# A gated attention and state-space mix on one core: an emission order planned with the matrix engine's instruction blocks, half of a Hankel table copied by one DMA, and earlier keys

## The chip, the cores and the metric

The kernel runs on one core of one Trainium2 chip. The time is that of one execution on the device, in microseconds (us). A profile is one further execution, recorded by the hardware profiler. The engines are called as the profile calls them: PE is the matrix engine (PEld its weight loads), DVE the vector engine, ACT the scalar engine, POOL the general engine, SP the engine that only issues transfers.

## What is computed

Two branches read the same x (2048 rows of 448, bf16) and are mixed by a gate per row. Branch A is attention with 16 query heads of width 28 that share one key and one value head. Branch B is a state-space layer: a kernel K of length 2048 for each of 448 channels, made from 256 complex modes, convolved causally with x.

```
q = (x @ wq) per head;  k = x @ wk;  v = x @ wv
a = softmax(q k^T * 28**-0.5) v, heads joined, @ wo
P = exp(dt*A*l) for l in 0..2047
K[d,l] = Re sum_n C[d,n] P[d,n,l] dt*B[d,n]
b = causal_conv(K, x) per channel + x * Dskip
out = g*a + (1-g)*b,  g = sigmoid(x . gate_w)
```

## The kernel before

**Order.** The code doesn't write its instructions in the order in which they run. Each call of `op` or `dma` records an operation with a guess of its duration, its dependences and a priority `pr` (smaller goes first). `schedule` then plays a list schedule: again and again it takes, of all operations whose inputs are there, the one that can start earliest by the guesses, and appends it to its engine's list. `emit` writes the lists out and puts semaphore waits where one engine needs another. So a guess that changes moves instructions on every engine, and an engine never overtakes its own list: an instruction that waits holds up all that stand behind it.

**Attention.** There are 1024 score tiles: 16 blocks of queries i (4 heads of one group by 512 queries) times 16 key tiles times 4 heads. A tile is 128 keys by 512 queries in one PSUM bank. The tiles go in sets of 3 and 2 by turns over five banks (`main`, `sets`). For each set PE makes the scores, ACT takes the exponential of the whole set from PSUM into a ring of 15 tiles in SBUF (`expT`, L1115), and PE multiplies them with the values (`pv`, L1125). A set's scores come in one of two forms. In the row form (L1084) a tile is one matmul over 29 rows of the array, from qT. In the full form (L1093) a tile is four matmuls over 128 rows and 32 columns each, from qM, a copy of qT in which each head has its own 32 rows and the rest are zero; POOL issues the four DMAs that fill it. Before, sets of 3 use the row form, sets of 2 the full form, and block i = 0 the row form throughout, so that no qM is made for it.

**Query shift.** `prep_x` transposes x, makes the keys kT in four quarters q (PE, then ACT at L587, then a maximum on DVE at L590), and from the four maxima the bias matrix Wb (L607, L609). Each `qproj(i)` needs Wb for its last matmul (L750), so the first scores wait for the fourth quarter of kT. The transposed x of quarters 2 and 3 lies in qM until it is stored to a scratch tensor; POOL then clears qM (L605).

**State space.** `masters` and `tables` build powers of the modes on DVE for groups of 32 channels (14 groups c); the last operation of a group's table is L854. `kgen(c)` is 128 small matmuls (L871) on PE; DVE copies the result (L881, L884), and POOL stores it to the scratch tensor KP by nine DMAs. `tload` loads Toeplitz blocks of KP, 1 MiB for a group index gi (0 to 111), four DMAs of 256 KB each from SP, into seven buffers (four in T, three in the part of U that is used up). `conv` (L930, two of them for a group, each over four gi) multiplies them with U; DVE takes the result out (L939), PE turns it (L950), DVE adds it to O (L958). U holds x in a Hankel form for all 128 partitions; it is assembled from x by DMAs into a staging buffer in O and 16 copies on POOL (L520). PE's fillers `kgen`, `conv` and the turns have priorities 1.7, 1.6 and 1.55 and go between the score sets. A filler (`ni` set and `pr` at least 1) is held back when the instructions issued lately are over BURST.

**End.** After the last exponential come the normalisation of block 15 (L985, L1003 to L1018), the last output projections (L1036, added to O at L976), what is left of `conv`, and the stores of O, which stand behind the last table load on SP.

## Time and profile before

| what | us |
| --- | --- |
| median of 3 runs (566.47 to 568.52) | 567.91 |
| the profiled execution, time | 568.51 |
| its span, first to last instruction | 566.6 |
| ACT busy in the span | 487.0 (86%) |
| PE busy | 469.7 (83%) |
| DVE busy | 462.3 (82%) |
| POOL busy | 174.1 (31%) |

A line of the profile gives line, engine, operation and tile, then how often, the busy time and the mean of one in ns, and after the last bar the idle time of the engine just before these instructions with what ended most of it. In a timeline, the two first numbers are start and length, and the bracket at the end is the idle time before, with what ended it. "issue" there means that the engine waited for nothing that the profile shows.

### The profile page before, as it was taken

To read this page: it belongs to the slowest core of one execution; us is meant where nothing else is said; L and a number is where in the kernel's file an instruction comes from. 1 tells how busy PE (TensorE), PEld (TensorE's weight loads), DVE (VectorE), ACT (ScalarE), POOL (GpSimd) and SP (SyncE) were. 2 spreads that over 40 slices of the span, in tenths; PEclk is the share of its full clock that TensorE was granted. 3 is DMA by queue.
4 is the path that set the end of the run, shared out by engine and by line. 5 is a ranking of instruction groups with operands and counts; after the bars stand their busy time and mean duration, and the time that the engine had idled before them with its cause. 6 is when DMAs were issued, how large, how long until landed. Compare 5 with 4: busy or idle time off the path is not lost.

```text
span 566.6 us, 20978 instructions
## 1 busy us (share of the span) xinstructions
PE 469.7 (83%) x9383; PEld 228.7 (40%) x9383; DVE 462.3 (82%) x826; ACT 487.0 (86%) x431; POOL 174.1 (31%) x317
## 2 busy tenths in 40 slices
PE   5678878879779989799887999879878999889772
PEld 4522112315325444434444443534424453545351
DVE  4877999999889999799898999879898997871230
ACT  3779999999899999799898999879998997999700
POOL 2026531512414233044323352142321450152200
PEclk8855578879889999999899999989999997999985
DMA  8932251187369899979899599957989499868998
GB/s 256 219 86 74 67 141 45 30 309 228 116 202 294 279 346 290 309 259 308 272 356 301 189 352 307 349 191 242 321 273 347 123 360 359 305 187 296 357 386 271
DMA packets 92322, 141.68 MB, mean 250 GB/s; under 512 B 23156, under 2 KB 30940, under 8 KB 92232
## 3 DMA queue, kind: packets, MB, share of 16 engines
q1 hardware_dynamic: 82360, 130.32, 69.3%
q0 software_dynamic: 9216, 9.46, 6.8%
q8 instruction: 73, 1.20, 0.9%
q10 hardware_dynamic: 656, 0.57, 0.4%
q14 instruction: 17, 0.14, 0.1%
HBM read 129.68 MB, written 5.28 MB: 238 GB/s over the span
## 4 chain that ended last, share of the span: by engine, by line
ACT 52%; PE 30%; DMA 6%; issue 5%; DVE 3%; SPq 3%; ACTq 0%
ACT expT L1115 51%; PE psS L1093 5%; PE psS L1084 5%; PE psB L1125 4%; SPq L134 3%; PE psX L871 3%; DMA U<-KP_scratch 2%; DMA T<-KP_scratch 2%; PE psS L871 2%; PE psS L930 2%; PE psX L930 2%; PE psS L741 1%; DMA seedw<-in_gate_w_dram 1%; PE psS L1036 1%; PE psX L950 1%
## 5 line engine op out<-in xcount | busy, mean ns | idle before, releaser
L1115 ACT ACTIVATE expT<-psS 128x1536 bf16<-128x1536 f32 (+1 forms) x410 | 468.8, 1304 | 34.8 <-PE psS L1084 21.7
L1093 PE MATMUL psS<-qM,kT 128*32 128x512 bf16 x1532 | 126.9, 406 | 11.4 <-ACT expT L1115 9.7
L1084 PE MATMUL psS<-qT,kT 29*128 29x512 bf16 x641 | 94.8, 422 | 32.1 <-ACT expT L1115 27.8
L1125 PE MATMUL psB<-expT,vaug 128*32 128x512 bf16 x1024 | 111.2, 416 | 5.3 <-issue 3.4
L134 POOL DMA_DIRECT2D KP_scratch<-kstg x126 | 67.7, 545 | 78.3 <-DVE kstg L884 71.5
L832 DVE TENSOR_TENSOR tab<-tab,mbf 128x2048 bf16<-128x2048 bf16 (+4 forms) x70 | 68.5, 979 | 1.0
L1084 PEld LDWEIGHTS psS<-qT,kT 29*128 29x128 bf16 x641 | 21.6, 92 | 92.0 <-ACT expT L1115 78.4
L1125 PEld LDWEIGHTS psB<-expT,vaug 128*32 128x32 bf16 x1024 | 27.8, 96 | 62.8 <-issue 49.1
L134 POOL DMA_DIRECT2D rdenB<-R_scratch x60 | 29.9, 504 | 54.6 <-DMA R_scratch<-denT 44.3
L1093 PEld LDWEIGHTS psS<-qM,kT 128*32 128x32 bf16 x1532 | 29.2, 99 | 40.3 <-ACT expT L1115 30.3
L871 PE MATMUL psS<-tab 128*32 128x64 bf16 x1024 | 41.1, 287 | 5.1 <-issue 4.9
L930 PE MATMUL psS<-T,U 128*26 128x128 bf16 (+7 forms) x1408 | 34.2, 228 | 6.9 <-DMA T<-KP_scratch 4.8
L871 PE MATMUL psX<-tab 128*32 128x64 bf16 x768 | 33.0, 286 | 8.0 <-issue 7.9
L134 POOL DMA_DIRECT2D qM<-qT x60 | 30.3, 513 | 25.4 <-DVE qT L753 12.2
L834 DVE TENSOR_TENSOR tmp<-tab,mbf 128x256 bf16<-128x256 bf16 (+3 forms) x56 | 36.1, 644 | 0.0
L930 PE MATMUL psX<-T,U 128*26 128x128 bf16 (+7 forms) x1376 | 34.3, 225 | 1.9 <-issue 1.8
L871 PEld LDWEIGHTS psS<-tab 128*32 128x32 bf16 x1024 | 30.5, 135 | 13.3 <-issue 7.2
L134 POOL DMA_DIRECT2D denT<-acc x15 | 11.7, 782 | 73.4 <-DVE acc L985 73.4
L930 PEld LDWEIGHTS psS<-T,U 128*22 128x22 bf16 (+7 forms) x1408 | 26.4, 97 | 19.4 <-DMA T<-KP_scratch 5.9
L849 DVE TENSOR_TENSOR tab<-tab,tmp 128x4096 bf16<-128x4096 bf16 x14 | 32.0, 2288 | 0.3
L834 DVE TENSOR_TENSOR tab<-tab,mbf 128x4096 bf16<-128x4096 bf16 x14 | 31.9, 2281 | 0.0
L930 PEld LDWEIGHTS psX<-T,U 128*26 128x26 bf16 (+7 forms) x1376 | 26.5, 97 | 13.2 <-issue 5.0
(155 smaller groups left out, 591.6 us busy)
## 6 DMA issues: line engine op xcount, KB each, us to landing
T<-KP_scratch SPq DMA_DIRECT2D x348, 256.0 KB, 5.7
U<-KP_scratch SPq DMA_DIRECT2D x100, 256.0 KB, 5.7
rdenB<-R_scratch POOLq DMA_DIRECT2D x60, 64.0 KB, 5.0
qM<-qT POOLq DMA_DIRECT2D x60, 32.0 KB, 5.0
tab<-in_A_x_dram SPq DMA_DIRECT2D x4, 448.0 KB, 5.9
O<-in_A_x_dram SPq DMA_DIRECT2D x16, 112.0 KB, 2.6
O<-cst SPq DMA_DIRECT2D x1, 1792.0 KB, 9.3
KP_scratch<-kstg POOLq DMA_DIRECT2D x112, 16.0 KB
```

The costliest lines, as they stand in the source:

```text
L134: return [e.dma_start(o, i, **kw) for o, i in pairs]
L741: pg.op("pe", lambda e, T=T: e.matmul(px(), self.Wq.v(0, DT, T * 512 + g * 128, [[1, 128]]), self.xT.v(0, DT, T * 512, [[1, 512]]), start= ...
L832: vo(lambda e, dst=dst, src=src, mr=mr: e.tensor_tensor(dst, src, mr, ALU.mult), 2 * n, done + mk(lv), [kr, ki])
L834: vo(lambda e, src=src, mi=mi, w=w, tb=tb, to=to: e.tensor_tensor(tb.v(0, P, to, [[w * EW, 2], [EW, w], [1, EW]]), src, mi, ALU.mult), 2 * ...
L849: vo(lambda e: e.tensor_tensor(tab.v(0, P, FM, [[64, 2], [EW, 32], [1, 64]]), tab.v(0, P, lo + 31 * EW, [[BLK, 2], [-EW, 32], [1, 64]]), r ...
L871: r = e.matmul(G.v(32 * g, 32, 64 * jj, [[1, 64]]), tab.v(0, P, lo + comp * BLK + 64 + o, [[EW, 32]]), tab.v(0, P, fo, [[mo - fo, 2], [EW, ...
L930: r = e.matmul(ps.v(32 * j, 32 - 2 * n, 128 * k, [[1, 128]]), self.U.v(0, P, (4 * gi + j) * 32 + 2 * n, [[1, 32 - 2 * n]]), tbuf.v(0, P, t ...
L950: r = e.matmul(px.v(64 * par, 64, 64 * k, [[16, 4], [1, nt]]), self.cst.v(0, P, cs * 512 + 128 * k + 64 * (1 - mu), [[1, 64]]), self.ident ...
L1084: r = e.matmul(self.psS.v(0, P, 512 * b, [[1, 512]]), kT.v(32 * h, DH + 1, 128 * kt, [[1, 128]]), qT.v(32 * h, DH + 1, 512 * (i % 2), [[1, ...
L1093: r = e.matmul(self.psS.v(32 * j, 32, 512 * b, [[1, 512]]), kT.v(0, P, 128 * kt + 32 * j, [[1, 32]]), self.qM.v(0, P, (i % 2) * XQ + 512 * ...
L1115: pg.op("act", lambda e: e.activation(expT.v(0, P, 512 * es[0], spread(es, n)), self.psS.v(0, P, 512 * bs[0], spread(bs, n)), AF.Exp, scal ...
L1125: r = e.matmul(self.psB.v(32 * h, 32, 0, [[1, 512]]), vaug.v(0, P, 32 * kt, [[1, 32]]), expT.v(0, P, 512 * ring[t], [[1, 512]]), start=(kt ...
```

## The change

The planner's guesses change. PE's instructions are counted (a matmul is two: weight load and multiplication), and an instruction of block j of 256 can't start before that block has been fetched; a fetch starts when PE enters the block before it, and takes 5300 ns while DMAs run and 3300 ns otherwise. Fillers are further held back so that the scores behind them don't run dry. PE's durations are multiplied by 1.8 between 21 and 45 us of the plan. Transfers get a new cost formula, and one exponential of `prep_params` a longer duration.

```diff
-    BURST, FETCH = 250, 4000.0
+    BLOCK, FIRST, FETCH, IDLE, NEED = 256, 172, 5300.0, 3300.0, 0.015
+    HALF = (21000.0, 45000.0, 1.8)
...
-                    if o.ni and o.pr >= 1:
...
+                    if e == "pe":
+                        j = (npe + o.ni - self.FIRST - 1) // self.BLOCK + 1
+                        if j < len(block):
+                            r = max(r, block[j])
+                            if o.pr >= 1 and block[-1] > r:
+                                left = self.FIRST + (len(block) - 2) * self.BLOCK - npe - o.ni
+                                r = max(r, block[-1] - left / self.NEED)
...
+            if e == "pe":
+                npe += o.ni
+                while npe > self.FIRST + (len(block) - 2) * self.BLOCK:
+                    block.append(r + (self.FETCH if dmafree > r else self.IDLE))
```

The work itself changes in five places. The upper half of U (64 of the 128 partitions) is no longer loaded and copied but taken from the lower half by one DMA of 28,672 pieces of 32 bytes; POOL's copies fall from 16 to 8, and all of U is first cleared by one DMA. The transposed x of quarters 2 and 3 lies in the ring `expT`, so qM is cleared by POOL at the very start. qM is made for block 0 as well; the first six sets use the row form, sets 6 to 13 the full form, and the later ones the old rule (3 row, 2 full). The keys get priority -2, ahead of the sines of `prep_params`. `kgen` gets priority 1.4, ahead of `conv` and the turns. Each gi of `tload` is loaded by two DMAs of 512 KB (the even and the odd partitions) in place of four.

```diff
+        for k in range(2):
+            pm(V(self.qM, k * XQ, XQ), 0.0, 1800, [("qM", k)], 1.5)
...
+        self.late.append(pg.dma([(V0(self.U, 0, 32 * D, 64), Z(32 * D, 64))], (8192, 448), "zU", rd=[("cst", 1)],
+                                wr=[("U", k) for k in range(4)] + uc, pr=0.25).i)
         for k in range(2):
...
+        half = lambda o: bass.AP(tensor=self.U.h, offset=o, ap=[[2 * rs, 64], [32, D], [1, 16]])
+        pg.dma([(half(rs + 16), half(0))], (28672, 32), "du", rd=[("U", 0), ("U", 1)],
+               wr=[("U", 2), ("U", 3)] + uc, pr=0.35, slow=True)
...
-                rd=[("b", b), "s0"], wr=[("kT", q)])
+                rd=[("b", b), "s0"], wr=[("kT", q)], pr=-2)
...
-            if q >= 2:
-                pg.op("pool", lambda e, xT=xT, xo=xo: e.memset(xT.v(0, P, xo, [[1, XQ]]), 0.0), 2500,
-                      wr=self.xk(q) + [("qM", q % 2)], pr=1)
...
-        return ((self.xT, 0), (self.T, NTR * TW + 768 - XQ), (self.qM, 0), (self.qM, XQ))[q]
+        return ((self.xT, 0), (self.T, NTR * TW + 768 - XQ), (self.expT, 9 * 512), (self.expT, 5 * 512))[q]
...
-        if i:
+        if True:
...
-                      wr=[X, "kst", "kst2"], pr=1.7, lock=G if jj == 0 and comp == 0 else None)
+                      wr=[X, "kst", "kst2"], pr=1.4, lock=G if jj == 0 and comp == 0 else None)
...
-        for j in range(4):
-            lst.append((buf.v(0, P, o + 1024 * j, [[1, 1024]]), dram(self.KP, (4 * gi + j) * KW, [[1, 64], [KH, 2], [1, 1024]])))
+        for h in range(2):
+            to = bass.AP(tensor=buf.h, offset=h * buf.rs + o, ap=[[2 * buf.rs, 64], [1024, 4], [1, 1024]])
+            lst.append((to, dram(self.KP, h * KH + 4 * gi * KW, [[1, 64], [KW, 4], [1, 1024]])))
...
-            if len(ts) == 3 or dec(ts[0])[0] == 0:
+            if s < 6 or s >= 14 and len(ts) == 3:
```

**Where it moves instructions.** The changed file has 18 or 19 more lines ahead of these places, so its line numbers are higher by that much. First ACT's list around the first exponentials, before: L698 and L699 are the sines, L587 is the fourth quarter of the keys, L706 the decay factors mq, L1115 the exponentials of the scores.

```order
L698 ACTIVATE T<-T 128x896
L699 ACTIVATE T<-T,small 128x896
L703 ACT_TABLE_LOAD
L703 ACTIVATE mbf<-T 128x896
L587 ACTIVATE kT<-psS,small 128x512
L618 ACTIVATE gt<-psB 128x16
L706 ACTIVATE mq<-T 128x2x14x32 x5
L1115 ACTIVATE expT<-psS 128x1536
```

The same place now:

```order
L716 ACTIVATE T<-T 128x896
L606 ACTIVATE kT<-psS,small 128x512
L717 ACTIVATE T<-T,small 128x896
L721 ACT_TABLE_LOAD
L721 ACTIVATE mbf<-T 128x896
L636 ACTIVATE gt<-psB 128x16
L724 ACTIVATE mq<-T 128x2x14x32 x3
L1134 ACTIVATE expT<-psS 128x1536
L1134 ACTIVATE expT<-psS 128x1024
L1134 ACTIVATE expT<-psS 128x1536
L724 ACTIVATE mq<-T 128x2x14x32
```

The fourth quarter of the keys has moved ahead of the second sine, a table load and an exponential, and two of the five mq now stand behind the first exponentials. Next PE's list where the first `kgen` (L871) begins, before: L1084 and L1093 are scores, L1125 the product with the values, L741 and L750 the next query block.

```order
L741 MATMUL psX<-xT,Wq 128x512
L871 MATMUL psS<-tab 32x64 x8
L1084 MATMUL psS<-qT,kT 128x512 x3
L1125 MATMUL psB<-expT,vaug 32x512 x4
L871 MATMUL psS<-tab 32x64 x8
L1093 MATMUL psS<-qM,kT 32x512 x8
L750 MATMUL psX<-qT,Wb 128x512
L871 MATMUL psS<-tab 32x64 x16
```

The same place now:

```order
L889 MATMUL psS<-tab 32x64 x8
L1112 MATMUL psS<-qM,kT 32x512 x8
L1144 MATMUL psB<-expT,vaug 32x512 x4
L889 MATMUL psS<-tab 32x64 x24
L1103 MATMUL psS<-qT,kT 128x512 x3
L1144 MATMUL psB<-expT,vaug 32x512 x4
L889 MATMUL psS<-tab 32x64 x8
L1112 MATMUL psS<-qM,kT 32x512 x8
L889 MATMUL psS<-tab 32x64 x32
```

Counted over the whole list, the first `kgen` began behind 130 score tiles and now begins behind 108; the last one (c = 13) ran from tile 975 to 995 and now runs from 940 to 955; each ends 25 to 47 tiles sooner, and takes 12 to 18 tiles where it took 15 to 32. Last DVE's list from the normalisation of block 15 on, before: L1007 to L1018 belong to it, L976 adds the output projection to O, L939 and L958 take one `conv` out.

```order
L1007 RECIPROCAL denT<-psS 128x16
L1009 COPY rdenB<-denT 128x512
L1018 TENSOR_TENSOR onT<-acc,psS 128x512
L976 SCALAR_TENSOR_TENSOR O<-psS,gt,O 128x448 x2
L939 TENSOR_TENSOR cst<-psX,omq 128x512
L976 SCALAR_TENSOR_TENSOR O<-psS,gt,O 128x448 x2
L958 TENSOR_TENSOR O<-O,psX 128x16x16
L939 TENSOR_TENSOR cst<-psS,omq 128x512
L958 TENSOR_TENSOR O<-O,psX 128x16x16
L939 TENSOR_TENSOR cst<-psS,omq 128x512
L958 TENSOR_TENSOR O<-O,psX 128x16x16
```

The same place now:

```order
L1026 RECIPROCAL denT<-psS 128x16
L1014 TENSOR_TENSOR onT<-acc,rdenB 128x512
L1028 COPY rdenB<-denT 128x512
L1037 TENSOR_TENSOR onT<-acc,psS 128x512
L995 SCALAR_TENSOR_TENSOR O<-psS,gt,O 128x448 x2
L958 TENSOR_TENSOR cst<-psS,omq 128x512
L995 SCALAR_TENSOR_TENSOR O<-psS,gt,O 128x448 x2
L977 TENSOR_TENSOR O<-O,psS 128x16x16
L958 TENSOR_TENSOR cst<-psX,omq 128x512
L977 TENSOR_TENSOR O<-O,psS 128x16x16
```

Three convolutions were taken out behind the last normalisation; now it is two. On PE, ten gi of `conv` stood behind the normalisation's first matmul, and six do now.

## Prediction

> **What bounds the kernel now.** I read the page's chain first, then ACT by stages, then ACT's timeline.

> ```profile
> ACT 52%; PE 30%; DMA 6%; issue 5%; DVE 3%; SPq 3%; ACTq 0%
> L1115 ACT ACTIVATE expT<-psS 128x1536 bf16<-128x1536 f32 (+1 forms) x410 | 468.8, 1304 | 34.8 <-PE psS L1084 21.7
> ```

> The exponentials carry the chain and have 34.8 us of idle time ahead of them. By stages (second number: length; then busy time of PE, PEld, DVE, ACT and POOL):

> ```profile
> 33.00:67.00 34.00, 30.34 (x162) 8.30 (x157) 28.16 (x48) 30.01 (x26) 16.83 (x18) 0.50 0.31 82
> 96.00:300.00 204.00, 177.31 (x3767) 85.72 (x3770) 188.74 (x351) 193.17 (x171) 65.64 (x122) 0.94 0.79 256
> 300.00:508.00 208.00, 182.04 (x4099) 91.85 (x4095) 183.41 (x318) 190.44 (x167) 68.73 (x128) 0.97 0.84 279
> 535.00:566.60 31.60, 16.98 (x404) 12.05 (x403) 8.54 (x15) 0.00 (x0) 0.00 (x0) 0.69 0.97 335
> ```

> ACT idles 4.0 us in the first stage, 10.8 and 17.6 (208.00 - 190.44) in the long ones, and does nothing in the last 31.6. There the transfers run at 0.97. Now the ends of ACT's work:

> ```profile
> 33.13 2.36 ACT L1115 ACTIVATE expT<-psS 128x1536 bf16<-128x1536 f32 x2 [1.87 <-PE psS L1084]
> 496.43 36.27 ACT L1115 ACTIVATE expT<-psS 128x1536 bf16<-128x1536 f32 x32 [1.07 <-PE psS L1084]
> 532.92 1.94 ACT L1115 ACTIVATE expT<-psS 128x1536 bf16<-128x1536 f32 x2 [0.22 <-PE psS L1084]
> ```

> 32 sets of 3 and 2 by turns are 80 tiles in 36.27 us: 0.453 us a tile, which no edit changes. 1024 tiles are 464 us. So the span is 33.1 (until the first exponential) + 464 + about 37.7 of idle + 31.7 after 534.9. The change can work on the first, third and fourth.

> **Start.**

> ```profile
> 21.99 0.95 ACT L698 ACTIVATE T<-T 128x896 f32<-128x896 f32 x1 [0.98 <-DVE T L695]
> 26.33 0.67 ACT L587 ACTIVATE kT<-psS,small 128x512 bf16<-128x512 f32 x1
> 26.96 4.30 ACT L706 ACTIVATE mq<-T 128x896 bf16<-128x896 f32 x5
> ```

> The fourth quarter of the keys moves from 26.33 to right behind the first sine, 21.99 + 0.95 = 22.94: 3.4 us sooner. From it a serial path (maximum, Wb, bias matmul, qT, scores) led to 33.13; with it, the first exponential comes at 29.7. ACT itself is then free: its work ahead is the same without two mq, 31.26 - 1.72 = 29.5. Those two, 0.86 each, now stand between exponentials. Gain 3.4 - 1.7 = 1.7. If DVE holds up the path as before, nothing is gained and the two mq cost 1.7; the ends are -3.4 and +1.7.

> **POOL's copies and the tables.**

> ```profile
> 46.56 0.29 DVE L650 COPY omq<-psX 128x128 f32<-128x128 f32 x1 [2.09 <-PE psX L645]
> 46.72 8.06 POOL L520 COPY U<-O 128x896 bf16<-128x896 bf16 x7
> 48.09 1.00 DVE L780 SCALAR_TENSOR_TENSOR seedz<-seedz 128x128 f32<-128x128 f32 x1
> 55.30 0.29 DVE L780 SCALAR_TENSOR_TENSOR seedz<-seedz 128x128 f32<-128x128 f32 x1
> 95.16 0.69 DVE L854 TENSOR_SCALAR tab<-tab 128x1984 bf16<-128x1984 bf16 x1
> 96.14 0.42 PE L871 MATMUL psS<-tab 128*32 128x64 bf16 x8
> ```

> The same DVE operation takes 1.00 us beside a copy and 0.29 without one, so a copy costs DVE 0.71. Eight fewer give 5.7 us (4 to 6, by how many fall beside busy DVE). DVE is the path here: PE began `kgen` at 96.14, as soon as L854 ended at 95.85. The operations on DVE up to there are the same in number. With the 3.4 us of the earlier keys, the first table is ready 9 us sooner, near 87; if PE's delay at L650 also goes, 11.

> `kgen(0)` stands 22 tiles sooner. ACT comes to tile 108 at 29.7 + 1.7 + 4.0 (idle, as before) + 108 x 0.453 = 84.3. So PE will wait for the table there for up to 2.5 us; the five banks of scores hide about 2. I take 1, inside the idle term below.

> **The long stretch.** Two kinds of waits hold it:

> ```profile
> SPq L134 <- DMA KP_scratch<-kstg: 109.2, 12, 37.4
> DVE kstg L881 <- PE psX L871: 11.5, 5, 4.2
> DVE kstg L881 <- PE psX L930: 7.4, 2, 5.3
> DVE kstg L881 <- PE psS L871: 4.2, 2, 3.3
> PE psX L871 <- issue: 7.9, 7, 1.9
> PE psS L871 <- issue: 4.9, 3, 1.9
> PE psB L1125 <- issue: 3.4, 4, 1.7
> PE psS L1084 <- ACT expT L1115: 27.8, 62, 0.7
> PE 469.7 (83%) x9383; PEld 228.7 (40%) x9383; DVE 462.3 (82%) x826; ACT 487.0 (86%) x431; POOL 174.1 (31%) x317
> q8 instruction: 73, 1.20, 0.9%
> ```

> SP waits 109 us for stored results of `kgen`: the tables pace the convolutions, not the transfers. DVE waits 23.1 us in order for `kgen` to end, with the next table queued behind; 5.3 of that lies in the tail. PE stands still for 16.2 us behind nothing that shows, in runs of small matmuls (the three "issue" rows); 73 instruction transfers over 2 x 9383 = 18,766 PE instructions are one per 257. So the rows support blocks of 256 that run dry.

> What the new order can give ACT is bounded by 28.4 (10.8 + 17.6) and zero. The upper bound by DVE: the last table was ready at 508.8, and PE's `kgen(13)` now stands at tile 940.

> ```profile
> 508.14 0.68 DVE L854 TENSOR_SCALAR tab<-tab 128x1984 bf16<-128x1984 bf16 x1
> ```

> ACT is there at 534.9 - 84 x 0.453 - 1.7 - G = 495.1 - G, with G the idle time saved; the table is there at 508.8 - 9.1 - W = 499.7 - W, with W the DVE waits saved. So G can't exceed W - 4.6. `kgen` takes 15 tiles where it took about 25, ten tiles or 4.5 us less, which ends most of the 17.8 us of DVE's waits: W near 13.6, G near 9. I take 9.

> [...]

> **Tail.**

> ```profile
> 520.16 0.67 DVE L884 CAST kstg<-psS 128x504 bf16<-128x504 f32 x1
> 521.14 4.78 POOL L134 DMA_DIRECT2D KP_scratch<-kstg  x9 [5.51 <-DVE kstg L884]
> 531.34 5.57 SPq L134 DMA_DIRECT2D T<-KP_scratch  x8
> 536.11 1.50 PE L1003 MATMUL psS<-msq,acc 128*128 128x4 f32 x8 [0.80 <-DVE acc L985]
> 546.35 1.39 DVE L976 SCALAR_TENSOR_TENSOR O<-psS,gt,O 128x448 bf16<-128x448 f32 x2
> 550.61 3.48 SPq L134 DMA_DIRECT2D T<-KP_scratch  x4
> 562.11 0.42 DVE L958 TENSOR_TENSOR O<-O,psX 128x256 bf16<-128x256 bf16 x1 [0.74 <-PE psX L950]
> ```

> Behind the last exponential the loads still run until 554.1, two gi in 5.57 us, 2.8 each. Ten gi stood behind L1003; six do now: 4 x 2.8 = 11. The reason must hold too: the last `kgen` result went to KP from 521.14; it ends 40 tiles (18 us) sooner in ACT's time, so the eight gi that need it can all be on their way by ACT's end. What is late next is the normalisation: it ended at 547.7, 12.9 after ACT's end, and 4 us of stores follow (562.5 to 566.6), so 17 is the floor of a tail of 31.7. The gain lies between 0 (loads late as before) and 14.7; I take 11.

> The loads' new form halves SP's instructions. The pieces stay 2 KB, so their transfer is costed at nothing; the tail's 0.97 share says the engines, not SP, would stay the limit. If the larger strides cost a tenth, the tail's eight gi would lose 2 us.

> **The copy of U.** Nothing like 28,672 pieces of 32 bytes is in the trace. The nearest rows:

> ```profile
> out_dram<-O SPq DMA_DIRECT2D x1, 128.0 KB, 3.6
> q0 software_dynamic: 9216, 9.46, 6.8%
> 44.58 2.15 POOL L134 DMA_DIRECT2D qM<-qT  x4 [11.12 <-DVE mbf L798]
> qM<-qT POOLq DMA_DIRECT2D x60, 32.0 KB, 5.0
> ```

> The store of 128 KB is 2048 pieces of 64 bytes, 128 for each of 16 engines in 3.6 us with all latency: at most 28 ns a piece. By that the copy takes 1792 x 28 = 50 us, surely less. It starts when POOL, which first issues qM (44.58 + 2.15), has made 8 copies at 1.15 (8.06 / 7): at 56. Its reader, `conv(0)`, stands behind tile 170, at 29.7 + 1.7 + 4.0 + 77.0 = 112. So the cover is 56 us and hides it; queued behind it on SP are the clearing of O and all loads, none needed before. The dear end is the mean packet of q0: 6.8% of 566.6 x 16 us over 9216 is 67 ns, 120 us in all.

> [...]

> The clearing of all U falls where transfers run at 0.31 (33 to 67) and is hidden. The full form in sets 6 to 13 needs qM early: POOL issues it once qT is there, some 1.5 us ahead of the first exponential, and it takes 2.15 + 5.0 us, so 35; tile 15 comes at 29.7 + 1.7 + 15 x 0.453 = 38. Its 60 extra matmuls meet a PE that is busy 30.3 of 34 us at a clock of 0.50; if they don't fit into the 3.7 us left, ACT loses some 2 us, and if a fuller array lifts the clock (0.97 later on), it wins as much. I take nothing.

> **Sum.** 568.5 (the profiled execution, 1.9 outside the span, 0.6 over the median) - 1.7 - 9 - 11 = 546.8; against the median, 546.

> **The rivals.**
> 1. *Supply isn't what ACT waits for*, or the stalls only move: for it, 27.8 us of PE's own waits are for ACT; against, the gaps of 1.9 us in runs of L871. G = 0: 568.5 - 1.7 - 11 = 555.8.
> 2. *The order runs ahead of the tables.* `kgen` is at the head of PE's list, the table isn't ready, and all scores behind it wait. With W = 0 the wait at tile 940 is 4.6 us, G is nil, and half the tail's gain goes: 568.5 - 1.7 + 4.6 - 5.5 = 566, no change. For it, L854 ended only 0.3 us ahead of `kgen(0)`; against, DVE's 17.8 us.
> 3. *The copy of U is dear.* PE stops in order at `conv(0)` until it lands. It shows above 56 / 1792 = 32 ns a piece, and the whole is slower by over 0.5% from (56 + 22 + 3) / 1792 = 45 ns. At 67 ns it ends 64 us late: 546 + 64 = 610. For it, the packets of q0; against, the store of 64-byte pieces.
> 4. *All of it works*, G = 20: 536.

> **Chances.** Forecast (540 to 552) 0.50; rival 1 (552 to 562) 0.24; rival 4 (below 540) 0.10; rival 2 0.09; rival 3 0.07. The range 537 to 562 leaves out rivals 2 and 3 and the end of 4. A measurement here can tell about 0.5% (2.8 us) from no change: faster 0.84, same 0.08, slower 0.08 (rival 3 and a bad part of 2).

> **What would show it.** First exponential at 29.7; first table's last operation near 87, and POOL's copies over by 56; the copy of U landed before 106; ACT idle between 96 and its end down from 28 to about 19, with L871's "issue" rows and DVE's kstg waits shrunk; the last load issued within about 8 us of ACT's end. I am wrong if ACT's idle time stays, if PE's waits for L854 grow past 5 us, or if the tail behind ACT stays above 27.

## The result, and the profile after

The changed kernel takes **545.8 us** (median of 4 runs, 544.7 to 546.3) where the kernel before takes 567.8 (566.5 to 568.5): a ratio of 0.961, 95% interval 0.959 to 0.964, or 22 us less. The ratios, here and below, leave out executions over 1.5% longer than the fastest of the same kernel (as 558.8 us beside 550.3 of a_loads4). The profiled executions are 546.33 us with a span of 544.5, and 568.51 with a span of 566.6, so their spans differ by the same 22.1.

First the chain and the exponentials' group from the page of the changed kernel (lines are higher by 18 or 19 than in the kernel before: L1134 is the exponential, L1103 and L1112 are the scores, L889 is `kgen`, L949 `conv`, L872 a table's last operation).

```profile
ACT 30%; PE 27%; DVE 19%; DMA 15%; issue 3%; SPq 0%
L1134 ACT ACTIVATE expT<-psS 128x1536 bf16<-128x1536 f32 (+1 forms) x410 | 468.1, 1317 | 23.1 <-PE psS L1112 11.7
```

The exponentials are as long as before (468.1 beside 468.8), their idle time fell from 34.8 to 23.1, and ACT's share of the chain from 52 to 30%: DVE and the transfers have become links of it. By stages (second number: length, then busy time of PE, PEld, DVE, ACT and POOL, granted clock, share of the transfers):

```profile
33.00:67.00 34.00, 25.88 (x252) 7.87 (x251) 31.68 (x73) 31.35 (x28) 10.90 (x12) 0.80 0.67 129
96.00:300.00 204.00, 172.23 (x3922) 86.01 (x3929) 193.19 (x347) 197.06 (x173) 69.89 (x131) 0.99 0.83 273
300.00:508.00 208.00, 184.09 (x4170) 94.18 (x4180) 172.03 (x302) 196.85 (x174) 68.48 (x126) 0.98 0.90 301
```

ACT idles 2.7, 6.9 and 11.2 us there; it was 4.0, 10.8 and 17.6. The two ends, from ACT's timeline:

```profile
30.54 3.69 ACT L1134 ACTIVATE expT<-psS 128x1536 bf16<-128x1536 f32 x3
514.52 8.72 ACT L1134 ACTIVATE expT<-psS 128x1536 bf16<-128x1536 f32 x8 [0.99 <-PE psS L1103]
```

The first exponential comes 2.6 us sooner. The last one ends at 514.52 + 8.72 = 523.24 (534.86 before), and 544.5 - 523.24 = 21.26 us follow (31.74). So the 22.1 us are 2.6 in front, 9.0 between the first and the last exponential (492.7 us beside 501.7, though two mq have moved in there), and 10.5 behind.

The first tables, POOL's copies and the copy of U (DVE, POOL, SP):

```profile
44.88 4.67 POOL L535 COPY U<-O 128x896 bf16<-128x896 bf16 x4 [0.19 <-DMA O<-in_A_x_dram]
50.42 4.60 POOL L535 COPY U<-O 128x896 bf16<-128x896 bf16 x4 [0.86 <-DMA O<-in_A_x_dram]
55.04 0.64 SPq L135 DMA_DIRECT2D U<-U  x1
82.76 0.69 DVE L872 TENSOR_SCALAR tab<-tab 128x1984 bf16<-128x1984 bf16 x1
83.50 0.42 PE L889 MATMUL psS<-tab 128*32 128x64 bf16 x8 [0.16 <-DVE tab L872]
U<-U SPq DMA_DIRECT2D x1, 896.0 KB, 20.8
```

The first table is ready at 83.45, 12.4 us sooner, and PE waits 0.16 us for it. The copies are over at 55.0, and the copy of U has landed at 55.04 + 20.8 = 75.9. Now the waits of SP, DVE and PE (us, times, longest):

```profile
SPq L135 <- DMA KP_scratch<-kstg: 70.4, 7, 25.7
DVE cst L958 <- PE psX L949: 18.5, 8, 9.6
DVE kstg L899 <- PE psX L889: 6.9, 2, 6.7
PE psS L949 <- DMA T<-KP_scratch: 6.7, 6, 1.8
PE psX L949 <- DMA T<-KP_scratch: 5.9, 5, 2.0
PE psX L889 <- issue: 0.2, 1, 0.2
```

Waits for `kgen` are much shorter: on DVE 23.1 us became 7.2 (6.9 and a row of 0.3), on SP 109.2 became 70.4, and PE's unexplained waits ahead of `kgen`, 12.8 us, became 0.2. What has grown in their place is PE's wait for table loads (12.6 us here). DVE waits for `conv` (L958) as long as before: the row above and one of 5.2 us, 23.7 together, beside 12.2 and 10.8 (L939). Last, the tail, from the last `kgen` store on (POOL, SP, PE and DVE):

```profile
485.91 4.80 POOL L135 DMA_DIRECT2D KP_scratch<-kstg  x9 [13.38 <-DVE kstg L902]
524.38 1.24 SPq L135 DMA_DIRECT2D T<-KP_scratch  x2
524.49 1.05 PE L1022 MATMUL psS<-msq,acc 128*128 128x4 f32 x8 [0.18 <-DVE acc L1004]
532.13 0.69 DVE L1037 TENSOR_TENSOR onT<-acc,psS 128x512 bf16<-128x512 f32 x1 [5.29 <-PE psS L1033]
540.61 0.42 DVE L977 TENSOR_TENSOR O<-O,psS 128x256 bf16<-128x256 bf16 x1 [0.55 <-PE psS L969]
```

The last `kgen` starts on its way to KP 35 us sooner than before (521.14), and the last load is issued 1.1 us behind the last exponential, where it was 15.7 (550.61 behind 534.9).

### The profile page after: what moved, and what is told of

The parts are those of the page before. It is cut to its first block, busy times and chain, and to the rows that moved or that the text cites. A ratio compares the mean times of both kernels' runs of the same rounds, so it can differ in the third digit from the quotient of the medians.

```text
span 544.5 us, 20905 instructions
## 1 busy us (share of the span) xinstructions
PE 451.6 (83%) x9463; PEld 226.4 (42%) x9479; DVE 455.3 (84%) x826; ACT 485.9 (89%) x431; POOL 168.1 (31%) x313
## 3 DMA queue, kind: packets, MB, share of 16 engines
q1 hardware_dynamic: 112312, 133.06, 75.9%
## 4 chain that ended last, share of the span: by engine, by line
ACT 30%; PE 27%; DVE 19%; DMA 15%; issue 3%; SPq 0%
ACT expT L1134 30%; DMA T<-KP_scratch 9%; PE psS L1112 6%; DMA U<-KP_scratch 6%; PE psX L889 5%; PE psS L1103 4%; PE psB L1144 4%; PE psS L949 2%; PE psX L949 2%; DVE msq L796 2%; DVE tab L850 2%; DVE mbf L816 2%; DVE seedz L800 1%; PE psS L889 1%; DVE tmp L852 1%
## 5 line engine op out<-in xcount | busy, mean ns | idle before, releaser
L1134 ACT ACTIVATE expT<-psS 128x1536 bf16<-128x1536 f32 (+1 forms) x410 | 468.1, 1317 | 23.1 <-PE psS L1112 11.7
L1112 PE MATMUL psS<-qM,kT 128*32 128x512 bf16 x1660 | 134.3, 400 | 14.0 <-ACT expT L1134 10.6
L1103 PE MATMUL psS<-qT,kT 29*128 29x512 bf16 x609 | 82.9, 400 | 33.4 <-ACT expT L1134 29.6
L850 DVE TENSOR_TENSOR tab<-tab,mbf 128x256 bf16<-128x256 bf16 (+4 forms) x70 | 68.6, 979 | 0.7
L1103 PEld LDWEIGHTS psS<-qT,kT 29*128 29x128 bf16 x609 | 19.9, 91 | 83.3 <-ACT expT L1134 72.9
L889 PE MATMUL psX<-tab 128*32 128x64 bf16 x1280 | 49.5, 286 | 0.3 <-issue 0.2
L1112 PEld LDWEIGHTS psS<-qM,kT 128*32 128x32 bf16 x1660 | 30.4, 98 | 45.6 <-ACT expT L1134 34.7
L889 PEld LDWEIGHTS psX<-tab 128*32 128x32 bf16 x1280 | 39.4, 135 | 11.3 <-issue 3.9
L949 PE MATMUL psX<-T,U 128*32 128x128 bf16 (+7 forms) x1568 | 34.4, 221 | 9.0 <-DMA T<-KP_scratch 5.9
L949 PE MATMUL psS<-T,U 128*32 128x128 bf16 (+7 forms) x1216 | 30.2, 222 | 9.5 <-DMA T<-KP_scratch 6.7
L949 PEld LDWEIGHTS psX<-T,U 128*32 128x32 bf16 (+7 forms) x1568 | 26.5, 94 | 20.3 <-DMA T<-KP_scratch 8.1
L949 PEld LDWEIGHTS psS<-T,U 128*32 128x32 bf16 (+7 forms) x1216 | 21.7, 95 | 21.0 <-DMA T<-KP_scratch 6.9
L863 DVE TENSOR_TENSOR tmp<-tmp,mq 128x64 bf16<-128x64 bf16 (+4 forms) x70 | 25.3, 361 | 1.2
(153 smaller groups left out, 553.4 us busy)
```

The source lines that it names most:

```text
L850: vo(lambda e, dst=dst, src=src, mr=mr: e.tensor_tensor(dst, src, mr, ALU.mult), 2 * n, done + mk(lv), [kr, ki])
L863: vo(lambda e, w=w, lv=lv: e.tensor_tensor(rho.v(0, P, (32 - 2 * w) * 64, [[64, w], [1, 64]]), rho.v(0, P, (32 - w) * 64, [[64, w], [1, 64]]),
L889: r = e.matmul(G.v(32 * g, 32, 64 * jj, [[1, 64]]), tab.v(0, P, lo + comp * BLK + 64 + o, [[EW, 32]]), tab.v(0, P, fo, [[mo - fo, 2], [EW, ...
L949: r = e.matmul(ps.v(32 * j, 32 - 2 * n, 128 * k, [[1, 128]]), self.U.v(0, P, (4 * gi + j) * 32 + 2 * n, [[1, 32 - 2 * n]]), tbuf.v(0, P, t ...
L1103: r = e.matmul(self.psS.v(0, P, 512 * b, [[1, 512]]), kT.v(32 * h, DH + 1, 128 * kt, [[1, 128]]), qT.v(32 * h, DH + 1, 512 * (i % 2), [[1, ...
L1112: r = e.matmul(self.psS.v(32 * j, 32, 512 * b, [[1, 512]]), kT.v(0, P, 128 * kt + 32 * j, [[1, 32]]), self.qM.v(0, P, (i % 2) * XQ + 512 * ...
```

## The experiments

Two theories. **A**: what counts is where `kgen` stands in the order, since the tables pace the loads and the loads the tail. **S**: what counts is the new model of PE's instruction blocks, which keeps PE from standing still. Smaller rivals are that the work itself (copies, load form, keys, form of the score sets) brings the gain, or that each order has its own luck.

Each kernel ran in 4 executions or more beside runs of the kernel before on its chip; the ratio, with its 95% interval, is to those. "Order" is the tile at which the last `kgen` ends, and the gi of `conv` behind the normalisation. The last three columns are from the profiled execution: time between the first and the last exponential less the exponentials themselves, how long behind the last exponential the last gi's load is issued, and what follows the last exponential.

| kernel | median | ratio | order | gaps | last load | tail |
| --- | --- | --- | --- | --- | --- | --- |
| before | 567.8 | 1 | 995, 10 | 32.9 | 15.7 | 31.7 |
| changed | 545.8 | 0.961 (0.959-0.964) | 955, 6 | 24.6 | 1.1 | 21.3 |
| a_kgen17 | 566.5 | 1.007 (1.002-1.012) | 1020, 14 | 27.3 | 21.9 | 41.6 |
| b_kgen14 | 559.3 | 0.990 (0.986-0.994) | 985, 14 | 23.2 | 23.5 | 39.0 |
| b_sup | 582.4 | 1.031 (1.024-1.039) | 1024, 16 | 28.8 | 33.3 | 50.0 |
| a_oldsup | 550.2 | 0.975 (0.965-0.984) | 960, 5 | 32.3 | -4.4 | 20.1 |
| a_fetch50 | 545.2 | 0.964 (0.961-0.968) | 968, 5 | 27.0 | -2.9 | 17.3 |
| a_fetch57 | 548.6 | 0.970 (0.967-0.973) | 938, 4 | 30.4 | -2.9 | 20.7 |
| a_half1 | 556.5 | 0.984 (0.977-0.991) | 975, 9 | 32.8 | 13.0 | 27.9 |
| a_u16 | 551.6 | 0.975 (0.969-0.980) | 980, 8 | 27.0 | 9.8 | 24.8 |
| a_row | 545.0 | 0.965 (0.959-0.970) | 970, 9 | 23.2 | 7.3 | 22.2 |
| a_kt0 | 545.1 | 0.965 (0.960-0.970) | 955, 6 | 25.3 | 1.2 | 20.2 |
| a_loads4 | 553.1 | 0.976 (0.970-0.982) | 958, 5.6 | 38.5 | -0.5 | 19.1 |
| a_loads4s | 546.1 | 0.968 (0.964-0.973) | 955, 6 | 25.9 | 2.2 | 20.0 |

On the chip of the first four experiments told here the ratios are to a kernel before of some 563 to 565 us, so there the ratios count and not the medians. The profiled executions of b_kgen14 and a_loads4 were 5.6 us longer than their medians, so their gaps and tails are not compared to a few us.

**a_kgen17: `kgen`'s priority back.**

```diff
-  wr=[X, "kst", "kst2"], pr=1.4, ...
+  wr=[X, "kst", "kst2"], pr=1.7, ...
```

> The changed kernel with kgen's priority back at 1.7, all else kept. The first kgen still stands at tiles 108 to 125, but the last one ends at 1020 in place of 955, and 14 gi of conv stand behind the last normalisation in place of 6. Theory A (kgen's place in the order is the gain): the tail grows by 8 gi of 2.8 us, 22, less what lies in the seven buffers already, so by 10 to 22, and ACT's idle time by 0 to 9: 556 to 575. Rival S (the instruction model) and rival W (the changed work: fewer copies, earlier keys, full form): the gain stays, 546 to 551.

Its ratio is 1.007: nothing of the gain is left. Of the 23 us between the two profiles 20.3 lie in the tail and 2.7 in the gaps. Its waits and its last load:

```profile
SPq L135 <- DMA KP_scratch<-kstg: 122.2, 11, 25.5
PE psS L1112 <- issue: 9.7, 6, 3.1
PE psS L889 <- issue: 2.6, 2, 2.4
PE psX L889 <- issue: 1.9, 3, 1.0
547.84 2.58 SPq L135 DMA_DIRECT2D T<-KP_scratch  x2
```

SP waits for stored tables again (122.2 us; 70.4 in the changed kernel) and issues the last load 23.5 us later than there. The instruction model is all in place, and PE still stands unexplained ahead of `kgen` for 4.5 us and ahead of scores for 9.7. A is borne out; S and W are not, for this edit leaves the model and the changed work as they are.

**b_kgen14: the same priority alone, in the kernel before.**

```diff
-  wr=[X, "kst", "kst2"], pr=1.7, ...
+  wr=[X, "kst", "kst2"], pr=1.4, ...
```

> The kernel before with kgen's priority 1.4 alone. kgen gets closer (145, 220, 295, ... 985 in place of 150, 240, 300, ... 995), yet 14 gi of conv stand behind the last normalisation in place of 10. Theory A in its simplest form (priority alone is the gain): ACT's idle time falls by 5 to 9: 559 to 563. Theory A with the tables as the limit (kgen can't stand earlier than DVE finishes the tables, and what conv loses goes into the tail): the idle time gained is given back by up to 4 x 2.8 = 11 us in the tail: 563 to 574. Rival S: no change, 566 to 570.

It takes 1.0% less than the kernel before (0.6 to 1.4). PE's waits ahead of `kgen` (L871) are nearly gone, 1.9 us where they were 12.8, with the old supply rule in force:

```profile
PE psX L871 <- issue: 1.7, 2, 1.0
PE psS L871 <- issue: 0.2, 1, 0.2
```

Both halves of the expectation came: the gaps shrink by some 10 us, and the tail grows by 7, with 14 gi behind the normalisation and the last load issued 23.5 us behind the last exponential. Priority alone is worth some 6 of the 22 us.

**b_sup: the new instruction model alone, in the kernel before.** (The edit is the first diff of the change, BLOCK to `block.append`, without its HALF line.)

> The kernel before with the new instruction model alone. In its order kgen gets later: the first one at tiles 130 to 150 as before, the last one ends at 1024 in place of 995, and 16 gi of conv stand behind the last normalisation in place of 10. Theory A: the tail grows by up to 6 x 2.8 = 17 us: 572 to 585. Rival S: ACT's idle time falls by about 9 us, and the 'issue' waits go: 553 to 561.

It took 582.4, 3.1% more. The waits that the model is about, ahead of `kgen` (L888 here), fell only from 12.8 to 8.1, and `kgen` came later, so that the tail is 50 us:

```profile
PE psX L888 <- issue: 5.9, 5, 2.4
PE psS L888 <- issue: 2.2, 3, 1.7
```

**a_oldsup: the old supply rule put back into the changed kernel.** (The same diff, reversed; HALF stays as the change has it.)

> The changed kernel with the old rule for the supply of instructions (BURST 250, 4000 ns) put back, all else kept. The order it gives is nearly the changed one: the first kgen still begins at tile 108, the last one ends at 960 (955 in the changed kernel), and 5 gi of conv stand behind the last normalisation (6). Theory A (the gain comes from kgen standing earlier and closer, whatever put it there): 543 to 548, within 0.5% of the changed kernel. Rival S (the model of the instruction blocks is what keeps PE from standing still): the 'issue' waits ahead of kgen come back, 16 us of them, and with them about the 9 us of ACT's idle time that I forecast as gain: 553 to 558.

Its median is 550.2, between the two theories. But here the ratio counts: 0.975 of 567.8 is 553.4, the near end of S's range. It is 0.013 above the changed kernel's, and the intervals all but touch (one ends at 0.964, the other begins at 0.965). The tail is as A says. The gaps are 32.3 us, as S says, but in an execution 3.6 above its median. The waits ahead of `kgen` (L884 here) did not come back:

```profile
PE psS L884 <- issue: 1.1, 1, 1.1
PE psX L884 <- issue: 0.7, 1, 0.7
```

**a_fetch50 and a_fetch57: other numbers in the new model.**

```diff
-    BLOCK, FIRST, FETCH, IDLE, NEED = 256, 172, 5300.0, 3300.0, 0.015
+    BLOCK, FIRST, FETCH, IDLE, NEED = 256, 172, 5000.0, 3300.0, 0.015
```

> The changed kernel with FETCH 5000 in place of 5300: the same model, an order moved about as much as the old supply rule moved it (last kgen ends at 968, 5 gi behind the last normalisation; 960 and 5 with the old rule, whose time was 550.2 with a tail of 20.1). Theory S (the model is worth 4 to 8 us of ACT's idle time by itself): idle 23 to 27, tail 19 to 21: 543 to 547. Rival N (every other order costs that much, the old rule is no worse than another number): idle 27 to 33: 548 to 554.

(5700.0 in the other.)

> The changed kernel with one number of the instruction model moved, FETCH 5700 in place of 5300. The work is the same; in the order the last kgen ends at tile 938 in place of 955, and 4 gi of conv stand behind the last normalisation in place of 6. Theory A (tail by the gi behind the normalisation, down to its floor near 17): tail 17 to 19, idle as now: 540 to 545, the fastest kernel so far. Rival N (ACT's idle time hangs on the luck of each order, some 5 us either way): 540 to 552 with the tail at 17 to 19 all the same.

5000 gave 545.2 with gaps of 27.0, on the edge of the two expectations. 5700, whose `kgen` stands soonest of all, gave 548.6: its ratio, 0.970, lies above the changed kernel's interval. That interval is of another chip, though: on the chip of this run a_loads4s, which has the changed kernel's own order, stands at 0.968 (0.964 to 0.973), so no difference in time is shown. Its tail is 20.7, and its gaps are 30.4 as rival N allowed. So a number of the model moves the gaps by 2 to 6 us, and the old rule by 7.7.

**a_half1: the planner's factor on PE back at 1.0.**

```diff
-    HALF = (21000.0, 45000.0, 1.8)
+    HALF = (21000.0, 45000.0, 1.0)
```

> The changed kernel with the factor on PE's guessed durations put back from 1.8 to 1.0: the work is the changed one to the last instruction, only the order differs. The first kgen begins at tile 123 in place of 108, the last one ends at 975 in place of 955, and 9 gi of conv stand behind the last normalisation in place of 6. Theory A (the tail is set by the gi behind the normalisation; the runs so far give 20.1, 21.3, 31.7, 39.0, 41.6 and 50.0 us for 5, 6, 10, 14, 14 and 16 gi, some 2.75 each): tail 29 to 30, ACT's idle time 0 to 4 more than the 24.6 of the changed kernel: 553 to 558. Rival W (the work itself: fewer copies, full form, earlier keys): 545 to 548.

It took 556.5: 11 us by one guess, with every instruction of the work as in the changed kernel. The first exponential came 3.9 us sooner (26.65), the first table 1.6 us later, and `kgen` 2.2 us later, and the first `kgen` stands 15 tiles later in the order:

```profile
84.37 0.69 DVE L872 TENSOR_SCALAR tab<-tab 128x1984 bf16<-128x1984 bf16 x1
85.71 0.61 PE L889 MATMUL psS<-tab 128*32 128x64 bf16 x16
540.21 1.25 SPq L135 DMA_DIRECT2D T<-KP_scratch  x2
```

All `kgen` up to the last end 10 to 25 tiles later in the order, and the last load goes out 13.0 us behind the last exponential. Rival W (the work itself) is out by 8 us.

**a_u16: 16 copies on POOL.** U is built as before, without the DMA from its lower half.

```diff
-        for k in range(2):
+        for k in (2, 3, 0, 1):
...
-        pg.dma([(half(rs + 16), half(0))], (28672, 32), "du", ...)
```

> The changed kernel with U built as before: 16 copies on POOL, no DMA from the lower half, all else kept. The order then has the first kgen at tile 123, the last one ends at 980, and 8 gi of conv stand behind the last normalisation. Theory A: tail 26 to 28, idle 0 to 4 more: 551 to 556, about as the kernel with the same work as the changed one and 9 gi behind the normalisation. Rival C (the copies cost DVE their 5.7 us on top of what the order allows for): the first kgen waits for the table by 3 to 6 us more, 556 to 562. If the copy of U in one DMA saved nothing: 545 to 548.

It took 551.6, within A's range. The copies run to 60.2, and the first table (L880 here) is ready at 87.3 in place of 83.45:

```profile
55.67 4.56 POOL L547 COPY U<-O 128x896 bf16<-128x896 bf16 x4 [3.54 <-DMA O<-in_A_x_dram]
86.63 0.69 DVE L880 TENSOR_SCALAR tab<-tab 128x1984 bf16<-128x1984 bf16 x1
```

The first exponential stood 1.1 us sooner here (29.47), so eight copies cost the first table 3.9 to 5 us. Rival C's extra wait did not come: PE began the first `kgen` at 87.38, as soon as the table was ready.

**a_loads4 and a_loads4s: four loads for a gi.** In the second the planner still counts two issues, so that all lists but SP's loads are the changed kernel's own.

```diff
-        for h in range(2):
+        for j in range(4):
...
-                free[e] = r + self.ISSUE[e] * o.ndma
+                free[e] = r + self.ISSUE[e] * (2 if o.ndma == 4 and e == "sp" and o.slot[0] == "T" else o.ndma)
```

(The last two lines are in a_loads4s alone.)

> The changed kernel with four loads of 256 KB for a gi in place of two of 512 KB, all else kept. The order is the same to a few tiles (last kgen ends at 958, 5.6 gi behind the last normalisation). If only bytes count, as I forecast: 544 to 548. If the issue on SP counts (four at 0.6 us are 2.5 us for a gi that takes 2.8 in the tail): 1 to 3 us in the tail, 547 to 550. If the larger strides of the two cost a tenth: 541 to 544.

> The changed kernel with four loads of 256 KB for a gi, while the planner still counts the issues of two, so that every engine's list is the changed kernel's own and only the load instructions on SP differ. The earlier run with four loads, whose order had moved by a few tiles, took 553.1 us beside 545.1 on the same chip, with 38.5 us of ACT without an exponential in its profile. Theory L (the form of the loads itself is worth the 8 us, by their later landing): 550 to 555, and PE waits more for loads. Rival O (the few moved places in the order did it; the form is worth 0 to 2 us, as I forecast): 544 to 548.

The first took 553.1, more than any theory of mine for it; the second 546.1, as the changed kernel. At a fixed order the form is worth nothing that can be told, though a load of 256 KB landed 6.0 us after its issue in a_loads4s, and one of 512 KB 9.3 in the changed kernel (medians):

```profile
T<-KP_scratch SPq DMA_DIRECT2D x348, 256.0 KB, 6.0
```

What a_loads4 lost came with the places that moved in its order.

**a_kt0: the keys' priority back.**

```diff
-                rd=[("b", b), "s0"], wr=[("kT", q)], pr=-2)
+                rd=[("b", b), "s0"], wr=[("kT", q)])
```

> The changed kernel with the keys' priority back at 0. PE, DVE, POOL and SP have the very order of the changed kernel; on ACT the second sine stands ahead of the last quarter of the keys again, and nothing else moves. It serves as a second measure of the changed kernel on this chip as well. If the keys set the first exponential, it comes 0.7 to 1 us later, and the whole is 0 to 1 us longer: 545 to 548. If the place of the keys in the order were worth the 3.4 us that I read from the trace: 549.

It took 545.1, no change. Its third and last quarter of the keys on ACT, and what follows:

```profile
18.49 0.69 ACT L606 ACTIVATE kT<-psS,small 128x512 bf16<-128x512 f32 x1 [0.89 <-PE psS L600]
23.54 0.67 ACT L606 ACTIVATE kT<-psS,small 128x512 bf16<-128x512 f32 x1
24.22 1.28 ACT L721 ACT_TABLE_LOAD   x1
```

and those of the changed kernel, with the last operation ahead of its first exponential (30.54):

```profile
20.36 0.69 ACT L606 ACTIVATE kT<-psS,small 128x512 bf16<-128x512 f32 x1 [0.89 <-PE psS L600]
24.19 0.67 ACT L606 ACTIVATE kT<-psS,small 128x512 bf16<-128x512 f32 x1
28.02 2.62 ACT L724 ACTIVATE mq<-T 128x896 bf16<-128x896 f32 x3
```

Counted from the third quarter, the last one comes at 5.05 us here, at 3.83 in the changed kernel and at 7.31 before (26.33 and 19.02). So the priority is worth 1.2, the second sine. The other 2.3 came without it: here too the last quarter stands ahead of a table load and an exponential (L721) that it stood behind before. The first exponential comes 10.5 us behind the third quarter here, 10.2 in the changed kernel and 14.1 before. In both new kernels it follows the last of the three mq without a gap, so that ACT's own list sets it and no longer the keys.

**a_row: block 0 all in the row form.**

```diff
-            if s < 6 or s >= 14 and len(ts) == 3:
+            if len(ts) == 3 or dec(ts[0])[0] == 0:
```

> The changed kernel with the old rule for the form of the sets: block 0 all in the row form, so that PE runs it at a granted clock near 0.5 (before) and not 0.8. In the order the first kgen begins at tile 115, the last one ends at 970, and 9 gi of conv stand behind the last normalisation. Theory A (only the order counts): tail 27 to 30, idle as in the run with the factor at 1.0, which had the same 9 gi and 556.5 us: 553 to 558. Rival F (the full form of the early sets and its clock are worth something of their own): ACT's idle time from 33 to 67 us, 2.7 in the changed kernel, rises to 4 or more, and the whole is 1 to 4 us beyond that: 556 to 561.

It took 545.0, no change, and fits neither expectation. From 33 to 67 us the clock is low again and PE busier, and yet ACT idles only 1.7 us; and with 9 gi behind the normalisation the tail is 22.2:

```profile
33.00:67.00 34.00, 28.66 (x173) 7.42 (x172) 31.68 (x74) 32.30 (x30) 13.42 (x17) 0.57 0.67 116
525.87 1.24 SPq L135 DMA_DIRECT2D T<-KP_scratch  x2
```

The last load is issued at 525.9, 7.3 us behind the last exponential. So it isn't the count of gi in PE's list that makes the tail, but when the last of their loads is issued: from 7 us on, the tail is that column plus 15 to 17 us (19.7 in a_kgen17); below 3 us it is 17 to 21, whatever the loads do. No version tried is faster than the changed kernel by more than the intervals.

## Why the prediction was right, point by point

The time was forecast at 546.0 and measured at 545.8, with terms of -1.7, -9 and -11 that measured -0.9 (2.6 less two mq of 0.86), -10.7 (9.0 and the same two mq) and -10.5. Behind the sum the steps stand as follows.

**Start.** The keys' path was read rightly: the last quarter came 3.8 us behind the third instead of 7.3, the 3.4 of the prediction. The first exponential came at 30.54 and not 29.7, with a start that was itself 1.3 us late in this execution (the first quarter at 11.91, 10.58 before); in a_loads4s, with the same order, it came at 28.19. So the -0.9 is known to a microsecond or two only. The edit named was the smaller part: a_kt0 shows that the priority moves only a sine, 1.2 us, and nothing of the time. The other 2.3 us are from the change's other edits; which of them was not tried.

**Tables.** Forecast near 87, and 85 if PE's delay also went; measured 83.45, 12.4 us sooner. Of these, 4.0 lie ahead of DVE's work on the first table (L778 began it at 46.77, L796 does now at 42.73): DVE's maximum over the last quarter of the keys stands 1.0 us sooner, and PE's delay at L650 is gone (2.1; L668 waits for nothing). The other 8.4 lie in that work itself. It is 82 operations before and 83 now, and their durations sum to 51.4 and 44.7 us, so 6.8 us are shorter operations. That is a little more than the 4 to 6 that I gave for eight copies; eight copies alone, in the order of a_u16, cost 3.9 to 5.

**Copy of U.** Rival 3 falls. The copy took 20.8 us with all latency, so at most 20.8 / 1792 = 11.6 ns a piece, under the cheap end of 28 and far from the 31 (56 / 1792; the prediction wrote 32) at which it would have shown. The path never waited for it: PE's first `conv` (L949) began at 112.2, 36 us behind the landing at 75.9.

**The long stretch.** The size came, its working only in part. Ahead of the last table DVE's waits for `kgen` fell from 17.8 to 0.5 us, where W was put at 13.6. The rest, 5.3 before and 6.7 now, stands behind the last table (and not in the tail, as the prediction says: the 5.3 end at 520.1, ahead of the last exponential). The order was in step with the tables, so rival 2 falls. But the bound G <= W - 4.6 was not the limit: the last table was ready at 476, 32 us sooner, not the 22.7 of the step. What is late next, and was not in the prediction, is the loads: PE's waits for T grew from 1.1 us to 12.6 between 33 and 535 us.

That blocks of 256 instructions run dry is right, and the traces show it more closely than the prediction did. Take each of PE's waits of over 0.6 us that the profile puts down to "issue", from 33 us on, and count all PE instructions ahead of it (a matmul is two). In the kernel before there are 15, and the count divided by 256 leaves 192 to 194 each time; each wait ends 1.3 to 1.7 us behind the end of a 16 KB transfer on the instruction queue. In the changed kernel the same holds for all 8, and in the 14 profiles together for all 137 (1.2 to 1.8 us). By count and transfer, then, PE waits there for its next block, whatever instruction comes first in it; "runs of small matmuls" in the prediction is too narrow, for its third row, L1125, multiplies 128x512. Three such rows of a_kgen17, which stand four and two blocks apart:

```profile
499.90 0.40 PE L1112 MATMUL psS<-qM,kT 128*32 128x512 bf16 x3 [2.02 <-issue]
526.31 0.62 PE L949 MATMUL psX<-T,U 128*32 128x128 bf16 x29 [1.46 <-issue]
541.42 0.45 PE L949 MATMUL psS<-U 128*26 128x128 bf16 x18 [1.75 <-issue]
```

The model's 5300 and 3300 ns for a fetch, and when it starts one, are the planner's guesses, which no run measured; where two blocks in a row came late in the kernel before (five times), the second began 5.6 to 6.8 us behind the first.

What does not stand is that the new model cures these waits, and what they cost. They don't go with the model: all "issue" waits of PE between 33 and 535 us are 12.5 us in b_kgen14 and 14.7 in a_oldsup, under the old rule with `kgen`'s new priority, 18.7 in b_sup and 25.4 in a_kgen17, under the new model without it, and 6.7 to 20.9 in the orders that have both. Those ahead of `kgen` go with its priority (1.9, 1.8, 8.1 and 4.5 us in the four). ACT's gaps do not follow them either: a_fetch57 has 6.7 us of them and gaps of 30.4, a_row 17.6 and 23.2. Rival 1 is thus right in its premise, that supply isn't what ACT waits for, and wrong in its price: the gaps shrank all the same. PE's unexplained waits between 33 and 535 us are 22.6 us before and 12.1 after, 2 to 4% of the span; of the 69 and 71 blocks that begin there, 15 and 8 cost over 0.6 us.

How much of the gaps each edit is worth can't be settled. Two runs with the same order on PE, DVE and POOL repeat the 24.6 us within 1.3 (25.3 and 25.9), so most of what follows belongs to the orders and not to chance. But seven orders under the new model, in profiles of the changed kernel and of kernels with one edit undone or moved, lie between 23.2 and 32.8, and the old rule's 32.3 lies within that. Whether the model is worth anything beyond the choice of one good order stays open.

**Tail.** The size was right (10.5 for 11), its working was not: 2.8 us for each gi behind the normalisation fits most of the orders to 2 us, and a_row breaks it by 7. What holds is the prediction's other reason, that the last `kgen` must reach KP early enough for the loads to be over. The last load's issue came 14.6 us closer to the last exponential, and the tail shrank by 10.5 of them. The normalisation was named as what is late next, with a floor of 17; the other orders whose last load is issued by 3 us behind the last exponential have 17.3 to 20.7, and 21.3 here.

**Which edit did it.** Undoing `kgen`'s priority takes away all 22 us, but alone it gives some 6, in an order whose first table comes 13 us later (at 96.4) and which leaves 14 gi behind the normalisation. The factor on PE's guesses (11 us when undone) and the eight copies (6 us) bring the first `kgen` 15 tiles forward, and the others with it. No run undoes the new cost formula of transfers, the longer guess for one exponential, or the new places of the transposed x and of qM's clearing. The form of the loads, the keys' priority and the form of the early sets show no change that these runs can tell.

## What to carry to other kernels

Where a planner makes the order, price an edit by the order that it gives, and test it at a fixed order as well: the same load form measured 8 us slower or nothing, by whether the order was let move. Look for the producer that paces a tail (here `kgen`, by SP's wait for its stores), and ask when its last result leaves; the length of the list behind it is only a sign. An edit that is worthless alone, or worse, may be needed by another, so undo parts from the finished kernel as well as adding them to the old one. When an engine's waits have no cause in the profile, count its instructions ahead of each: here one remainder by 256 told what 21 of 22.6 us of them were.
